# Filling the first microseconds of a transformer-block kernel: dummy matmuls, another load order, the first tile on VectorE, and two token tiles half by half

## The chip, the cores and the metric

The kernel runs on one core of one Trainium2 chip. The metric is the device time of one execution in microseconds (us). Each experiment was timed in five rounds beside the kernel before on the same chip, and it has a ratio with a 95% interval.

## The reference, cut to what matters

```python
h  = x + attention(layernorm(x))          # linear attention with phi(t) = (t + 1 if t > 0 else exp(t)) + 1e-6, then @ wo
h2 = h + (relu(gate) * up) @ W_down       # gate, up = layernorm(h) @ W_gate, W_up
# x: 1 x 2048 x 1024, wqkv: 1024 x 3072, 32 heads of 32, F = 3584, bfloat16
```

Only the first stage matters here: layer normalisation of the first token tiles, and `k = xn @ wk`, `v = xn @ wv` of the first four tiles.

## The kernel before: the parts that the change and the argument touch

A token tile is 128 tokens of 1024 features. Each is loaded, normalised (statistics on VectorE, the scaling on ScalarE), and transposed in eight 128x128 blocks on TensorE. The blocks come in two groups of four. VectorE evicts the first group from PSUM and ScalarE the second; both groups share one PSUM buffer, so the second waits for the first eviction.

```python
load_x(atiles[0])                 # 256 KB
load_w(wk_sb, 0, D)               # first 512 columns of the K weights, 1 MB
load_x(atiles[1])
load_w(wk_sb, 1, D)               # second 512 columns, 1 MB
load_x(atiles[2]); load_x(atiles[3])
for j in range(2):
    load_w(wv_sb, j, 2 * D)

def ln_T(t):
    ...                            # bn_stats x2, bn_aggr, rstd = exp(-0.5 ln(var + eps))
    nc.scalar.activation(out=xn[:], in_=x_sb[:], func=ACT.Identity, bias=nmr, scale=rstd)
    for k in range(2):
        pt = pspool.tile([P, KH, P], BF16, tag="D", bufs=1, name="tp")
        for kc in range(KH):
            nc.tensor.transpose(pt[:, kc, :], xn[:, (k * KH + kc) * P:(k * KH + kc + 1) * P], ident[:])
        (nc.scalar.copy if k else nc.vector.tensor_copy)(
            out=xT[s][i][:, k * KH:(k + 1) * KH, r:r + P], in_=pt[:])

def k_plain(t):
    for j in range(2):             # per column half: 8 matmuls of 128x512, then exp, min, max
        ...

ln_T(atiles[0]); ln_T(atiles[1])
for t in units[0]:                 # four tiles
    k_plain(t)
    ln_T(todo.pop(0))
for n, t in enumerate(units[0]):
    v_plain(t)
    ...
    if n == 1:
        sums_unit(1); k_sums()     # sums of weight blocks for a Strassen-like scheme used later
```

The text of the program isn't the order of the instructions: a scheduler orders each engine's work. It moves `k_sums`, which needs all K weights and nothing else, to the moment when those weights land. It is VectorE work of about 1.2 us per sum.

## Time and profile before

| | |
|---|---|
| median time, 4 runs | 769.04 us (768.19 to 771.18) |
| TensorE busy | 740.3 of 768.0 us |
| first transposes | 7.10 us |
| full rate reached | 14.66 us (first clock record of the trace) |
| first V matmul | 27.74 us |

The page's first part gives busy time of each engine, its share of the span, and instructions:

```profile
PE 740.3 (96%) x3584; PEld 340.2 (44%) x3584; DVE 482.0 (63%) x868; ACT 321.6 (42%) x593; POOL 6.1 (1%) x44
```

TensorE (PE) is the bound, so time can only be won where it idles or runs slowly. The table of waits for the first 32 us says what TensorE waited for (us in total, times, longest):

```profile
PE tp L265 <- ACT xn L258: 7.1, 1, 7.1
PE tp L265 <- DVE xT L266: 1.4, 1, 1.4
PE tp L265 <- ACT xT L266: 0.3, 1, 0.3
```

The timeline of TensorE from 0 to 29 us (start, duration, what, how many; in brackets the idle time before it and what ended it):

```profile
7.10 0.61 PE L265 MATMUL tp<-ident,xn 128*128 128x128 bf16 x4 [7.10 <-ACT xn L258]
9.11 0.58 PE L265 MATMUL tp<-ident,xn 128*128 128x128 bf16 x4 [1.41 <-DVE xT L266]
9.49 1.49 PE L313 MATMUL kp<-pq_mem,xT 128*128 128x512 bf16 x3
11.61 2.77 PE L313 MATMUL kp<-pq_mem,xT 128*128 128x512 bf16 x6
14.60 3.65 PE L313 MATMUL kp<-pq_mem,xT 128*128 128x512 bf16 x16
18.12 0.40 PE L265 MATMUL tp<-ident,xn 128*128 128x128 bf16 x4
27.74 1.46 PE L331 MATMUL vp<-wv_sb,xT 128*128 128x512 bf16 x6
```

Six K matmuls take 2.77 us from 11.61 on, and sixteen take 3.65 us from 14.60 on: the array first runs at half rate. The `tp` groups are the transposes. The matmuls from 18.36 to 27.7 us, left out here, follow each other without a gap.

What stands on VectorE when the second weights land (timeline of VectorE, 9.5 to 12 us), and the traffic of an early stretch (windows view: stretch, length, busy us and instructions of PE, PEld, DVE, ACT and POOL, then clock, DMA share, GB/s):

```profile
10.30 1.23 DVE L127 TENSOR_TENSOR pq_mem<-pq_mem 128x2048 f16<-128x2048 bf16 x1 [0.87 <-DMA pq_mem<-in_A_wqkv_dram]
```

```profile
3.50:6.00 2.50, 0.00 (x0) 0.00 (x0) 1.66 (x4) 0.60 (x3) 0.00 (x0) 1.00 1.09 375
```

The clock of that line, 1.00, isn't to be believed: the views print full rate wherever the trace has no clock record yet, and the first record comes at 14.66 us.

### The profile page before, as it was taken

Reading aid. Unit: us, or ns where it says so; the run is one execution under the profiler, and the core shown is the slowest. Engines: PE = TensorE matmul, PEld = TensorE weight load, DVE = VectorE, ACT = ScalarE, POOL = GpSimd, SP = SyncE. Lnnn points to the kernel's source line nnn. Section 1 sums busy time; section 2 is a strip of 40 time slices with the busy share of each in tenths; the row PEclk is TensorE's granted clock in tenths of the full one; section 3 lists DMA queues with packets and bytes.
Section 4 is the critical chain, followed back from the end, with each engine's and each line's share of the span. In section 5 each row is a group of like instructions: output and inputs, shape, how many; then the busy total and the mean of one; then the engine's idle time right before and its main releaser. Section 6 shows DMA issues by size and latency. Waiting matters only on the chain.

```text
span 768.0 us, 9610 instructions
## 1 busy us (share of the span) xinstructions
PE 740.3 (96%) x3584; PEld 340.2 (44%) x3584; DVE 482.0 (63%) x868; ACT 321.6 (42%) x593; POOL 6.1 (1%) x44
## 2 busy tenths in 40 slices
PE   5999999999889999999999999999998999999998
PEld 2444555444344444444444444444443444444443
DVE  5997654886896766656474564746545991349632
ACT  4775553877777554444444344444434000000000
POOL 0000000000000000000000000000000000000000
PEclk9999999999999999999999999999999999999999
DMA  9675003089767526154032140130001986971001
GB/s 321 145 138 150 1 1 110 1 186 225 180 154 192 121 63 209 45 152 131 7 87 72 34 131 8 55 103 29 28 7 60 331 261 209 316 256 49 28 27 55
DMA packets 125151, 89.76 MB, mean 117 GB/s; under 512 B 50352, under 2 KB 116912, under 8 KB 124592
## 3 DMA queue, kind: packets, MB, share of 16 engines
q1 hardware_dynamic: 125104, 89.15, 40.9%
q8 instruction: 28, 0.46, 0.2%
q14 instruction: 19, 0.16, 0.1%
HBM read 59.77 MB, written 17.83 MB: 101 GB/s over the span
## 4 chain that ended last, share of the span: by engine, by line
PE 64%; DVE 20%; ACT 8%; DMA 4%; issue 3%; SPq 0%; POOL 0%; DVEq 0%; ACTq 0%
PE A L596 16%; PE accA L759 11%; PE E L596 8%; PE accE L759 6%; PE attn L514 4%; DVE gu L615 4%; PE Aq L280 3%; PE Dp L596 3%; PE Aq L414 2%; PE Eq L280 2%; ACT snap L610 2%; PE Aq L629 2%; PE accD L759 2%; DVE stats L249 2%; DMA hn<-hn 1%
## 5 line engine op out<-in xcount | busy, mean ns | idle before, releaser
L615 DVE TENSOR_TENSOR gu<-E,snap 128x1024 bf16<-128x1024 f32 x48 | 58.7, 1223 | 90.1 <-ACT snap L610 87.5
L610 ACT COPY snap<-A 128x1024 f32<-128x1024 f32 x72 | 72.0, 1008 | 84.1 <-PE A L596 84.1
L759 PEld LDWEIGHTS <-hh 128*128 128x128 bf16 (+1 forms) x560 | 54.7, 98 | 67.7 <-issue 1.9
L617 ACT ACTIVATE gu<-gu 128x512 bf16<-128x512 bf16 x72 | 45.4, 630 | 86.2 <-DVE gu L615 85.9
L759 PE MATMUL accA<-wd,hh 128*128 128x512 f16 (+1 forms) x336 | 73.3, 379 | 1.4 <-DVE gu L615 1.4
L514 PE MATMUL attn<-wo_mem,oT 128*128 128x512 bf16 x256 | 59.3, 385 | 3.4 <-DVE o_sb L494 3.1
L596 PEld LDWEIGHTS <-tg 128*128 128x128 f16 x384 | 37.5, 98 | 49.5 <-issue 5.7
L596 PEld LDWEIGHTS <-tu 128*128 128x128 f16 x384 | 37.6, 98 | 45.3
L618 DVE TENSOR_TENSOR hh<-gu 128x512 bf16<-128x512 bf16 x72 | 30.5, 423 | 38.4 <-ACT gu L617 38.4
L147 ACT COPY u<-Aq 128x512 f32<-128x512 f32 x56 | 32.2, 581 | 44.5 <-PE Aq L280 20.9
L596 PE MATMUL A<-hn,tg 128*128 128x512 f16 (+1 forms) x192 | 49.3, 379 | 1.1 <-ACT snap L610 1.1
L596 PE MATMUL A<-hn,tu 128*128 128x512 f16 (+1 forms) x192 | 49.3, 379 | 0.0
L596 PEld LDWEIGHTS <-wg 128*128 128x128 bf16 x288 | 28.2, 98 | 34.5 <-issue 1.1
L596 PEld LDWEIGHTS <-wu 128*128 128x128 bf16 x288 | 28.2, 98 | 34.0
L514 PEld LDWEIGHTS <-oT 128*128 128x128 bf16 x256 | 25.2, 99 | 36.0 <-issue 8.6
L759 PEld LDWEIGHTS <-s 128*128 128x128 f16 x224 | 21.9, 98 | 27.2 <-issue 0.8
L615 DVE TENSOR_TENSOR gu<-Dp,snap 128x1024 bf16<-128x1024 f32 x24 | 29.3, 1220 | 2.3 <-PE Dp L596 2.3
L280 PEld LDWEIGHTS <-xT 128*128 128x128 bf16 (+1 forms) x192 | 18.6, 98 | 23.9 <-issue 2.4
L767 DVE TENSOR_TENSOR u<-accA,hres 128x512 f32<-128x512 f32 x16 | 10.8, 690 | 28.6 <-PE accA L759 28.1
L494 DVE TENSOR_TENSOR o_sb<-nd,rd 128x384 bf16<-128x384 f32 (+1 forms) x48 | 22.9, 508 | 8.6 <-ACT rd L493 8.3
L516 DVE SCALAR_TENSOR_TENSOR x_res<-attn,x_res 128x512 bf16<-128x512 f32 x32 | 22.0, 688 | 7.7 <-PE attn L514 7.6
L596 PE MATMUL E<-hs,tg 128*128 128x512 f16 x96 | 24.6, 378 | 0.9
(161 smaller groups left out, 1217.5 us busy)
## 6 DMA issues: line engine op xcount, KB each, us to landing
wd<-in_B_W_down_dram SPq DMA_DIRECT2D x16, 896.0 KB, 6.5
hh_dram<-hh SPq DMA_DIRECT2D x72, 128.0 KB, 1.7
wg<-in_B_W_gate_dram SPq DMA_DIRECT2D x14, 512.0 KB, 4.9
wu<-in_B_W_up_dram SPq DMA_DIRECT2D x14, 512.0 KB, 4.9
hh<-hh_dram SPq DMA_DIRECT2D x4, 1792.0 KB, 8.0
x_sb<-in_A_x_dram SPq DMA_DIRECT2D x16, 256.0 KB, 3.8
x_res<-in_A_x_dram SPq DMA_DIRECT2D x16, 256.0 KB, 3.0
h_dram<-x_res SPq DMA_DIRECT2D x16, 256.0 KB, 2.6
```

The source lines that it names most:

```text
L147: nc.scalar.copy(out=snaps[nm, v], in_=A[v][:])
L249: nc.vector.bn_stats(out=stats[:, k, :], in_=x_sb[:, k * NW:(k + 1) * NW])
L280: nc.tensor.matmul(ps[:], lhsT=left[m - 1][:, kc, r + v * P:r + (v + 1) * P], rhs=right[m - 1][:, kc, :], start=(start and kc == 0), stop= ...
L494: nc.vector.tensor_tensor(out=ov[:, c0:c0 + n], in0=ndv[:, :, 0:P].rearrange("p k (h e) -> p k h e", h=HPC), in1=rd[:, 0:n, :].unsqueeze(3 ...
L514: nc.tensor.matmul(ps[:], lhsT=st["oT"][:, c, :], rhs=wo_sb[:, c, j * NW:(j + 1) * NW], start=(c == 0), stop=(c == KC - 1))
L516: nc.vector.scalar_tensor_tensor(out=h_sb[:, j * NW:(j + 1) * NW], in0=ps[:], scalar=1.0, in1=h_sb[:, j * NW:(j + 1) * NW], op0=ALU.mult, ...
L596: nc.tensor.matmul(ps[:, v, :], lhsT=w[v][m - 1][:, kc, :], rhs=left[m - 1][:, kc, :], start=(start and kc == 0), stop=(kc == KH - 1), ski ...
L610: nc.scalar.copy(out=m[:], in_=ps[:])
L615: nc.vector.tensor_tensor(out=gu[:], in0=ps[:], in1=m[:], op=ALU.add)
L617: nc.scalar.activation(out=gu[:, 0, :], in_=gu[:, 0, :], func=ACT.Relu)
L618: nc.vector.tensor_tensor(out=d, in0=gu[:, 0, :], in1=gu[:, 1, :], op=ALU.mult)
L759: nc.tensor.matmul(accs[tt][:], lhsT=lhs[:, half * FD + f, tt * P:(tt + 1) * P], rhs=rhs[half][:, f, :], start=(start and half == 0 and f ...
```

## The change

Its intent: warm the array with dummy matmuls while the loads fly, have two token tiles on the chip before the weights, shorten the first tile's way by normalising it on VectorE in halves, and do tiles 0 and 1 column half by column half, so that the second weights are needed later. The core of the diff:

```diff
-        load_w(wk_sb, 0, D)
         load_x(atiles[1])
+        load_w(wk_sb, 0, D, KH)          # in two loads of 512 KB
         load_w(wk_sb, 1, D)
...
+            if t == atiles[0]:
+                for k in range(2):
+                    ks = slice(k * NW, (k + 1) * NW)
+                    nc.vector.tensor_scalar(out=xn[:, ks], in0=x_sb[:, ks], scalar1=mv[:, 0:1], scalar2=rstd,
+                                            op0=ALU.subtract, op1=ALU.mult)
+                transpose_in(t, xn)
+                return
...
-        ln_T(atiles[0])
+        with tc.high_priority():
+            zero = asmall.tile([P, NW], BF16, tag="zero", bufs=1, name="zero")
+            nc.vector.memset(zero[:], 0.0)
+            spin = pspool.tile([P, NW], FP32, tag="E", bufs=2, name="spin")
+            for n in range(SPIN):         # 14
+                nc.tensor.matmul(spin[:], lhsT=zero[:, 0:P], rhs=zero[:], start=True, stop=True)
+            ln_T(atiles[0])
         ln_T(atiles[1])
-        for t in units[0]:
-            k_plain(t)
-            ln_T(todo.pop(0))
+        first = [(t, (j,)) for j in range(2) for t in units[0][:2]] + [(t, (0, 1)) for t in units[0][2:]]
+        for t, js in first:
+            k_plain(t, js)
+            if js[0] or len(js) == 2 or t == units[0][1]:
+                ln_T(todo.pop(0))
```

More of the change, by code (lines that the diff above doesn't have):

```diff
@@ L74, in block_kernel @@
     PE_T = 4
+    SPIN = 14
     XB, HB = 3, 2
@@ L220, in load_x, with load_w @@
             x_tiles[t] = x_sb
-        def load_w(dst, j, col):
-            nc.sync.dma_start(out=dst[:, :, j * NW:(j + 1) * NW], in_=wqkv_v[:, :, col + j * NW:col + (j + 1) * NW])
+        def load_w(dst, j, col, step=KC):
+            for k in range(0, KC, step):
+                nc.sync.dma_start(out=dst[:, k:k + step, j * NW:(j + 1) * NW],
+                                  in_=wqkv_v[:, k:k + step, col + j * NW:col + (j + 1) * NW])
         def place(t):
@@ L261, in ln_T, with transpose_in @@
                 return
+            transpose_in(t, xn)
+        def transpose_in(t, xn):
+            s, i, r = place(t)
             for k in range(2):
@@ L303, in k_unit, with k_plain @@
             return token_unit(u, rk, fin)
-        def k_plain(t):
+        es = {}
+        def k_plain(t, cols):
             s, i, r = place(t)
-            new_pk(t)
-            e = bwork.tile([P, D], BF16, tag="o_sb", name="e")
-            for j in range(2):
+            if t not in pk:
+                new_pk(t)
+                es[t] = bwork.tile([P, D], BF16, tag="o_sb", name="e")
+            e = es[t]
+            for j in cols:
                 js = slice(j * NW, (j + 1) * NW)
```

## The prediction

> **What bounds the kernel now.** The page's engine table has TensorE busy 740.3 of 768.0 us (96%), VectorE 63%, so only TensorE's idle or slow time can be saved. The table of waits shows it at the start: 7.1 us before the first transpose, 1.4 and 0.3 us on evictions of transposes. The timeline adds that until about 14.2 us matmuls run slowly: six 128x512 K matmuls take 2.77 us from 11.61 (0.43 us apart), sixteen take 3.65 us from 14.60 (0.22). "TensorE: Matmul & The Clock Gate" of the Trainium skill (section on the clock gate) says the array runs at half rate until about 3.4 us of sustained work; this trace agrees. From 14.6 us TensorE is full until about 45 us; V starts at 27.74 us. By 14.6 it has done 9 K matmuls and 16 transposes, about 3.5 us at full rate: some 11 us is start-up loss. Not all can go: weights arrive at about 350 GB/s (windows view), first half near 7.2 us, second near 10.3 us (VectorE's first sum of weights starts then).
>
> **What the change does.**
> - 14 dummy matmuls from about 1 us: 8 slow (3.4 us), the rest fast, done by 6 to 7 us, in idle time. Worth up to 2 us of the slow part of 9.5 to 14.4, if the array stays warm through later gaps.
> - The second token tile lands near 4.4 instead of 7.2 us; weights as before.
> - First tile on VectorE: two halves of about 0.3 us (estimate from the 128x512 tensor_scalar, 0.29 us) for one ScalarE pass of 1.24 us. But the built order puts half a bn_stats of tile 1 (0.65 us) ahead of tile 0's aggregate, and ScalarE's 1.24 us pass for tile 1 ahead of its eviction of tile 0's second transposes. First transposes at about 6.6 us (7.1 before), first K matmuls at 8.5 (9.5 before).
> - Half by half does not fill the gap: in the built order three matmuls of tile 0's second column half stand before tile 1's first half. They wait for the second weights (10.3 us), and VectorE stands in its 1.23 us weight sum, also from 10.3, ahead of an eviction of tile 1's transposes. Tile 1's remaining transposes start near 12 us.
>
> I walked the built order with durations of the trace: tile 1's K work runs at full speed from about 12.4 to 16.9; tile 2 is transposed at about 17.3 (18.1 before), with 32 K matmuls done (25 before). Then tile 2's second transposes wait about 0.6 us on VectorE (a weight sum is in front), with no K matmul left as filler. V starts near 26.4 instead of 27.7: 1.3 us gained. VectorE is 97% busy from 40 to 60 us and gets 0.6 us more work, so a little may be given back. After that the order is nearly unchanged and the gain passes to the end.
>
> **Prediction.** 768.3 us, 1.2 us (0.2%) less; range 765.8 to 770.2. Chances: faster by over 2% 0.005, within 2% 0.99, slower by over 2% 0.005.
>
> **What would show it.** K matmuls 0.22 us apart from the first; first transposes at 6 to 7 us; a TensorE gap at about 11 to 12 us behind VectorE's sum or the second weights; another near 17 to 18.5 around tile 2; V starting at 26 to 27 us; TensorE waits after 60 us unchanged.
>
> **What would make it wrong.** The array cooling again at 6 to 12 us (1 to 2 us lost); VectorE giving all back by 60 us; or weights landing earlier, so that tile 1 isn't held up and 3 to 4 us are gained.

## The result, and the profile after

The changed kernel took 771.23 us in the median of 4 runs (769.93 to 771.85), against 769.04 us before. The ratio is 1.0023, interval [1.0005, 1.0041]: the same at 2%, and slightly longer where the prediction said 1.2 us shorter. The time lies outside the predicted range. (A ratio is the mean time of one kernel's runs over that of the other's of the same rounds, so it isn't quite the ratio of the medians that are quoted.)

TensorE's waits in the first 32 us, after:

```profile
PE tp L279 <- DVE xT L280: 1.9, 3, 0.9
PE kp L331 <- DMA pq_mem<-in_A_wqkv_dram: 1.7, 1, 1.7
PE spin L384 <- DVE zero L381: 1.2, 1, 1.2
```

The wait of 7.1 us for the first normalised tile is gone, and a wait of 1.7 us for weights is new. The timeline of TensorE shows where both led:

```profile
1.19 6.03 PE L384 MATMUL spin<-zero 128*128 128x512 bf16 x14 [1.19 <-DVE zero L381]
7.05 0.39 PE L279 MATMUL tp<-ident,xn 128*128 128x128 bf16 x4
8.17 1.03 PE L331 MATMUL kp<-pq_mem,xT 128*128 128x512 bf16 x4
9.41 1.03 PE L331 MATMUL kp<-pq_mem,xT 128*128 128x512 bf16 x4
12.12 0.81 PE L331 MATMUL kp<-pq_mem,xT 128*128 128x512 bf16 x3 [1.68 <-DMA pq_mem<-in_A_wqkv_dram]
13.78 0.58 PE L279 MATMUL tp<-ident,xn 128*128 128x128 bf16 x4 [0.86 <-DVE xT L280]
14.16 6.20 PE L331 MATMUL kp<-pq_mem,xT 128*128 128x512 bf16 x21
20.45 0.40 PE L279 MATMUL tp<-ident,xn 128*128 128x128 bf16 x4
21.36 0.38 PE L279 MATMUL tp<-ident,xn 128*128 128x128 bf16 x4 [0.52 <-DVE xT L280]
28.98 0.38 PE L349 MATMUL vp<-wv_sb,xT 128*128 128x512 bf16 x1
```

The first K matmuls run at full rate and 1.3 us earlier than before (8.17 against 9.49). Then TensorE idles from 10.44 to 12.12 us for the second weights, and from 12.93 to 13.78 us for an eviction on VectorE. Then 21 matmuls take 6.20 us. At the full-rate distance of 0.2155 us they would take 4.53; so about 1.67 us are lost while nothing is waited for. The windows view shows why, in its clock column (third from the right):

```profile
3.50:6.00 2.50, 2.50 (x7) 0.90 (x6) 2.50 (x6) 0.41 (x2) 0.00 (x0) 1.00 0.83 251
10.36:13.78 3.42, 0.89 (x4) 0.29 (x3) 1.61 (x3) 0.60 (x1) 0.00 (x0) 1.00 1.08 360
13.78:17.19 3.41, 3.41 (x12) 1.45 (x12) 3.20 (x7) 0.79 (x2) 0.00 (x0) 0.50 1.09 349
17.19:20.60 3.41, 3.32 (x18) 1.42 (x17) 2.34 (x6) 2.62 (x6) 0.00 (x0) 1.00 0.90 321
```

From 13.78 to 17.19 us the granted clock was 0.50. The 3.4 us before it held three K matmuls. The first line, from 3.5 to 6.0 us, shows another thing: the loads moved 251 GB/s there, against 375 before. And VectorE's first weight sum moved with the weights from 10.30 to 12.17 us. It still stands ahead of the eviction that TensorE needs at 12.93:

```profile
12.17 1.23 DVE L128 TENSOR_TENSOR pq_mem<-pq_mem 128x2048 f16<-128x2048 bf16 x1 [4.27 <-DMA pq_mem<-in_A_wqkv_dram]
13.31 0.42 DVE L280 COPY xT<-tp 128x512 bf16<-128x512 bf16 x1
```

V starts at 28.98 us, 1.24 us later than before. At 80 us the work as a whole lags by 1.15 us (starts of the same ScalarE and VectorE instructions in both traces), and at the end by 2.02. Of the further loss 0.3 us falls between 205 and 230 us, and 0.5 us near 270 us, where a wait of 1.5 us grew. The waits from 255 to 290 us, before and then after:

```profile
PE Aq L629 <- ACT m L147: 1.5, 1, 1.5
```

```profile
PE Aq L655 <- ACT m L148: 2.0, 1, 2.0
```

### The profile page after: what moved, and what is told of

It is laid out like the page before. It is cut to its first block, busy times and chain, and to the rows that moved or that the text cites. A ratio compares the mean times of both kernels' runs of the same rounds, so it can differ in the third digit from the quotient of the medians.

```text
span 770.0 us, 9640 instructions
## 1 busy us (share of the span) xinstructions
PE 746.0 (97%) x3598; PEld 341.7 (44%) x3598; DVE 482.1 (63%) x870; ACT 320.6 (42%) x592; POOL 5.9 (1%) x44
## 4 chain that ended last, share of the span: by engine, by line
PE 65%; DVE 19%; ACT 8%; DMA 4%; issue 3%; SPq 0%; POOL 0%; DVEq 0%; ACTq 0%
PE A L622 16%; PE accA L785 11%; PE E L622 8%; PE accE L785 6%; PE attn L540 5%; DVE gu L641 4%; PE Aq L294 3%; PE Dp L622 3%; PE Aq L440 2%; PE Eq L294 2%; PE Aq L655 2%; ACT snap L636 2%; PE accD L785 2%; DMA hn<-hn 1%; ACT hn L552 1%
```

## The experiments

I had these theories of the 2 us (and of the 3 us that were missing against the prediction):

1. The second weights land late because of the new load order (1.8 us late in the trace).
2. The clock: the array is put back to half rate for one window of 3.41 us.
3. The order: half by half leaves TensorE without work to put between transposes.
4. The order on VectorE: a weight sum stands ahead of an eviction.
5. Splitting the first weight load in two is what delays the loads.

(The expectations further down number their theories in their own way; go by what they say, not by the number.)

In the sixteen runs, "before + X" starts from the kernel before, "change - X" from the changed kernel. The table is the summary; times are medians, those of before from the same chip. "Second weights" is when the first and the last of that load's 16 parts landed in the profiled execution (from the semaphore updates in the packed trace; no view prints them).

| run | edit | us (before) | ratio, 95% | second weights, us | V starts |
|---|---|---|---|---|---|
| before | | 769.04 | 1 | 9.88 to 10.21 | 27.74 |
| the change | | 771.23 (769.04) | 1.0023 [1.0005, 1.0041] | 10.12 to 12.08 | 28.98 |
| again | the change, repeated | 768.82 (769.53) | 0.9993 [0.9975, 1.0010] | 11.05 to 11.58 | 26.82 |
| after3 | the change, repeated | 770.29 (769.59) | 1.0009 [0.9990, 1.0028] | 10.08 to 11.92 | 28.85 |
| nosplit | change - split load | 770.25 (769.53) | 1.0009 [0.9992, 1.0027] | 10.29 to 12.53 | 27.8 |
| nospin | change - dummies | 772.38 (769.53) | 1.0036 [1.0020, 1.0053] | to 12.20 | 30.2 |
| dve_order | change, weight sums held back | 772.03 (769.53) | 1.0030 [1.0011, 1.0048] | to 12.29 | 28.7 |
| b_spin | before + dummies | 767.32 (769.05) | 0.9973 [0.9956, 0.9991] | 9.81 to 10.24 | 25.58 |
| b_x1first | before + tile 1 ahead of the weights | 770.15 (769.05) | 1.0018 [0.9997, 1.0039] | 9.99 to 10.98 | 27.1 |
| fill | dve_order + 8 dummies | 773.14 (769.05) | 1.0056 [1.0034, 1.0079] | to 11.16 | 29.9 |
| xfirst2 | four token tiles first | 771.29 (769.05) | 1.0027 [1.0005, 1.0049] | to 12.24 | other order |
| oldload | change, old load order | 771.26 (770.13) | 1.0021 [1.0004, 1.0039] | to 10.31 | 26.63 |
| s_half | before + dummies + half by half | 770.63 (770.13) | 1.0017 [1.0000, 1.0034] | 9.88 to 11.10 | 28.6 |
| b_split | before + split load | 770.15 (770.13) | 1.0014 [0.9992, 1.0037] | 10.02 to 10.55 | 27.6 |
| whole | change - half by half | 769.08 (769.59) | 0.9996 [0.9981, 1.0012] | 10.69 to 12.61 | 28.86 |
| s_dve | before + dummies + VectorE tile | 768.41 (769.59) | 0.9984 [0.9970, 0.9999] | 9.89 to 10.23 | 25.57 |
| best | s_dve + two orders on VectorE | 767.41 (770.13) | 0.9969 [0.9953, 0.9986] | to 10.43 | 25.18 |
| best2 | best, repeated | 767.65 (769.59) | 0.9974 [0.9960, 0.9987] | 9.85 to 11.12 | 26.78 |

All outputs are right.

### The change again, unchanged: again and after3

> The changed kernel unchanged, to see what repeats. Theory 1 (the split of the first weight half upsets the transfers): the 16 parts of that load again land 1.5 to 2 us apart and the second weights again near 12 us. Rival: that was an accident of one execution, and the second weights land near 10.3 us as before. The array cooled once at 13.8 us for 3.4 us in the traced execution (mean clock 0.996) and two of four executions show 0.998 instead: I expect the same mixture, 0.996 executions about 1 to 1.7 us longer than 0.998 ones. Ratio to the kernel before 1.001 to 1.004.

> The change again, unchanged, beside the other three on one chip. It had 1.0023 and 0.9993 in two earlier sets. If the half-rate window near 14 us comes in some executions and not in others, its executions fall on both sides of 770 us, those with clock 0.996 about 1.5 to 2 us longer than those with 0.998; its mean lies 1 to 3 us above the best kernel's.

Three sets of the same kernel gave 1.0023, 0.9993 and 1.0009. The intervals overlap, so there is no contradiction, but the first set was the worst of the three. The 16 runs together have a median of 769.96 us and a mean of 770.0; the 44 runs of before in the four later sets have a mean of 769.5 (48 with those of the result, the same mean). So the change is about 0.5 us slower, or equal, and doesn't gain what was predicted.

The profiled execution of again had a clock of 1.000 and no half-rate window at all. Its TensorE timeline comes near to what was predicted:

```profile
11.62 0.81 PE L331 MATMUL kp<-pq_mem,xT 128*128 128x512 bf16 x3 [1.00 <-DMA pq_mem<-in_A_wqkv_dram]
13.28 0.38 PE L279 MATMUL tp<-ident,xn 128*128 128x128 bf16 x4 [0.86 <-DVE xT L280]
13.50 4.70 PE L331 MATMUL kp<-pq_mem,xT 128*128 128x512 bf16 x20
18.29 0.40 PE L279 MATMUL tp<-ident,xn 128*128 128x128 bf16 x4
19.20 0.38 PE L279 MATMUL tp<-ident,xn 128*128 128x128 bf16 x4 [0.52 <-DVE xT L280]
26.82 2.54 PE L349 MATMUL vp<-wv_sb,xT 128*128 128x512 bf16 x11
```

The same instructions in the same order: V starts 2.16 us earlier than in the other trace of this kernel. Of these, 1.67 us are the half-rate window, and 0.50 us are weights that landed at 11.58 instead of 12.08. Together that is 2.17. So theory 2 is shown for the trace of the result, by two executions of one kernel. In the times it shows as clusters: of the 16 runs the six with clock 1.000 took 768.6 us in the mean, and the four with 0.995 or 0.996 took 772.1. At clock 1.000 the 23 such runs of before took 768.8, so without half-rate windows change and before are alike within 0.2 us. The mean clocks of all runs are 0.9981 and 0.9989; the difference is worth about 0.7 us (an estimate, explained at theory 3), as much as the 0.5 us between the means.

One caution: the mean clock is that of the whole execution. Most of the traces, before's too, have one more half-rate window between 203 and 212 us, where TensorE idles for VectorE, and in again, s_half, b_split and best2 it didn't come.

Whether the window comes is partly luck, because the phase of the windows isn't tied to the program. "TensorE: Matmul & The Clock Gate" of the Trainium skill (Part 1, "What's actually happening") says that the window is 4096 cycles, about 3.41 us, and free-running. The traces agree: every half-rate stretch in the middle of a trace lasts 3.41 us, and with the same 14 dummies full rate came anywhere from 3.94 us (after3) to 7.14 us (whole).

### When the array is put back to half rate

Counting the work in each window of 3.41 us between the first full rate and about 25 us gives a table. I counted matmuls (0.215 us each) and transposes (0.055 us each, both as the starts at full rate lie apart), as shares of the window. These are all windows at full rate with less than 0.47 of matmuls:

| run, window (us) | matmuls | transposes | next window |
|---|---|---|---|
| dve_order 15.97 to 19.39 | 0.00 | 0.06 | half |
| fill 16.89 to 20.30 | 0.13 | 0.06 | half |
| nospin 11.01 to 14.42 | 0.13 | 0.06 | half |
| the change 10.36 to 13.78 | 0.19 | 0.00 | half |
| whole 10.55 to 13.97 | 0.19 | 0.00 | half |
| s_half 7.42 to 10.84 | 0.25 | 0.06 | half |
| best2 8.14 to 11.55 | 0.31 | 0.00 | half |
| nosplit 5.83 to 9.24 | 0.19 | 0.13 | half |
| after3 10.77 to 14.18 | 0.31 | 0.06 | half |
| b_spin 6.62 to 10.03 | 0.31 | 0.13 | full |
| xfirst2 4.70 to 8.11 | 0.31 | 0.13 | full |
| s_dve 6.96 to 10.37 | 0.31 | 0.13 | full |
| oldload 4.47 to 7.89 | 0.38 | 0.06 | full |
| five others | 0.44 | 0.06 to 0.13 | full |

By matmuls alone 0.31 stands on both sides. With the transposes counted, every window up to 0.37 was followed by half rate and every one from 0.44 on by full rate. This is a sorting of what was seen, not a test made for it, and the border isn't sharp. Counted in the same way to the end of all 18 traces, where TensorE has no transposes (matmuls narrower than 512 columns counted by their width), every window with up to 0.33 of matmuls led to half rate (twelve, all near 205 us) and every one from 0.41 on to full rate. But of those at 0.38 to 0.40, four led to half rate (after3 and whole near 205 us, oldload and best2 near 270) and nine to full. (A few matmul records are missing in the traces, so a share can be 0.06 too low.) Still, it says what the dummies buy: not a warm array for good, only full rate until the first window that's too empty. The page's section "Why this matters for your kernels" warns of idle gaps above about 3 us between bursts. Here gaps of 1.68 and 0.86 us, in one window of 3.41, were enough.

### Theories 5 and 1: nosplit, b_split, b_x1first

```diff
-        load_w(wk_sb, 0, D, KH)         # nosplit: the change, one load
+        load_w(wk_sb, 0, D)
```
```diff
-        load_w(wk_sb, 0, D)             # b_split: before, with the first weights in two loads of 512 KB
+        for k in range(0, KC, KH):
+            nc.sync.dma_start(out=wk_sb[:, k:k + KH, 0:NW], in_=wqkv_v[:, k:k + KH, D:D + NW])
```
```diff
-        load_w(wk_sb, 0, D)             # b_x1first: before, with tile 1 ahead of the weights
         load_x(atiles[1])
+        load_w(wk_sb, 0, D)
```

> First weight half loaded in one piece, still behind the second token tile. Theory 1 (the split delays weights): the second weights land at 10.3 to 10.6 us instead of 12.1, VectorE's first sum starts then, V starts 1 to 2 us earlier than 28.98, ratio to before 0.999 to 1.001. Rival (the split is innocent): landing near 12 us again and no change of V's start beyond 0.5 us.

> The kernel before with its first weight half loaded in two pieces, order otherwise as before. Theory 5 (what delays is small loads in front: a third load whose 16 parts are not all there when the first two, small ones, are through): the first two loads are now 0.25 and 0.5 MB instead of 0.25 and 1, through at about 4.4 us, so a spread of the parts between 0.5 and 1.5 us appears in the third load. Rival (only two token tiles in a row do it, or the split is harmless): spread stays below 0.5 us and second weights complete at 10.2 us. Ratio 0.999 to 1.002.

> The kernel before with the second token tile loaded ahead of the first weight half, in one piece, nothing else. Theory 1b (that order, not the split, makes the weights' 16 parts land 1.5 to 2.6 us apart): the last part of the first weights at 9 us or later (7.3 expected by bytes) and the second weights complete at 11.5 to 12.5 us (10.21 before); ratio to before 1.000 to 1.003. Rival (something else in the change does it): spread below 0.5 us and second weights at 10.2 us, ratio 0.999 to 1.000.

Without the split the second weights were as late as with it (12.53 us), and before with the split had them at 10.55. So theory 5 falls. With tile 1 in front the second weights' last part came at 10.98 instead of 10.21, and in all ten traces of kernels with two or more token tiles in front it came at 10.98 us or later, up to 12.61. In six of the eight with the old order it came at 10.21 to 10.55. But s_half and best2, in the old order, had 11.10 and 11.12; the order makes the delay likely and isn't its only cause. In time theory 1 isn't resolved: b_x1first has 1.0018, but its interval includes 1 and reaches 1.0039; whole and s_dve, which differ in the loads alone, have 0.9996 and 0.9984, overlapping; and oldload, with its second weights at 10.31, was no faster than the change.

In the trace of the result what is late is the last part, not the load as a whole: after the change the parts of the second weights land from 10.12 to 12.08 us, before from 9.88 to 10.21. In again, the same kernel, it is the load as a whole: its parts land close together, from 11.05 to 11.58. "DMA: Bandwidth & Descriptors" of the skill ("Queues, rings and completion order") says that a copy is split over up to 16 engines' rings and that completion isn't in order of issue. The traces agree in that each load has 16 parts that land on their own, up to 2.6 us apart (the first weights of nosplit from 6.94 to 9.52 us). What drives the parts apart when two small loads are in front stays open; no run here looked into it. From 6 to 17 us both kernels move 348 to 367 GB/s in the windows view, so what the change lost from 3.5 to 6.0 us isn't made good there.

### What the dummies do: nospin, b_spin

nospin takes these lines out of the change; b_spin puts only them into the kernel before:

```diff
+            zero = asmall.tile([P, NW], BF16, tag="zero", bufs=1, name="zero")
+            nc.vector.memset(zero[:], 0.0)
+            spin = pspool.tile([P, NW], FP32, tag="E", bufs=2, name="spin")
+            for n in range(14):
+                nc.tensor.matmul(spin[:], lhsT=zero[:, 0:P], rhs=zero[:], start=True, stop=True)
```

> No dummy matmuls, all else of the change. In this build the order on TensorE changes too: tile 1's first column half stands ahead of tile 0's second. Theory 2 (the dummies warm the array but make the scheduler order TensorE badly, so that a gap behind the second weights cools it again): slow matmuls until 13 to 15 us but no long gap, no second cooling, V starting at 27 to 29 us; ratio to before 0.999 to 1.003, so no worse than the whole change. Rival (dummies are worth their 2 us): 1 to 2 us slower than the whole change, 1.004 to 1.006.

> The kernel before with the 14 dummy matmuls alone. If the dummies are what helps: array at full rate by 5.3 to 7.2 us, second weights at 9.9 to 10.3 us as before, V starts at 26 to 27 us (27.74 before), ratio to before 0.998 to 0.9995. Rival (waiting for tiles takes it all back, or the array cools in a gap): V starts at 27.5 us or later, ratio 1.000 or more.

The dummies alone are worth 0.27%, about 2 us. The change without them is the slower by about as much (1.0036, against 1.0008 for the mean of the change's three sets), though its build orders TensorE's work differently too (tile 1's first column half ahead of tile 0's second), so that difference isn't the dummies' alone. The 2 us of b_spin are what the prediction allowed the dummies ("up to 2 us"). In b_spin the array is at full rate from 6.62 us on, and V starts at 25.58:

```profile
12.57 3.83 PE L313 MATMUL kp<-pq_mem,xT 128*128 128x512 bf16 x16
25.58 3.62 PE L331 MATMUL vp<-wv_sb,xT 128*128 128x512 bf16 x16
```

So one part of the change had the whole gain that one could hope for, and the others took it away again.

### Theory 4: dve_order and fill

```diff
+        evicted = {}                      # filled where VectorE evicts a tile's first transposes
...
-                k_sums()
+                with tc.issue_after(evicted[atiles[1]].ins):
+                    k_sums()
```

`issue_after` makes the scheduler place what it holds behind the given instruction on the engine. With it, the matmuls get the order on TensorE that the text of the change suggests: the first column half of both tiles ahead of the second. fill adds eight dummies behind tile 1's K work, to keep the array at full rate, and holds tile 2's transposes behind them (that hold isn't shown):

```diff
+                fill = pspool.tile([P, NW], FP32, tag="A", bufs=2, name="fill")
+                with tc.issue_after(mms["last"].ins):        # the last K matmul of tile 1
+                    for n in range(FILL):                    # 8
+                        mms["fill"] = nc.tensor.matmul(fill[:], lhsT=zero[:, 0:P], rhs=zero[:], start=True, stop=True)
```

> The whole change, with VectorE's first weight sum held behind its eviction of tile 1's first transposes. The build then puts tile 1's first column half ahead of tile 0's second, as the change meant. Theory 2: the gap of 3.3 us on TensorE between 10.4 and 13.8 us shrinks below 1.5 us, the array stays warm to 60 us, V starts at 26 to 27 us instead of 28.98, ratio to before 0.997 to 0.999. Rival (the loss is in the transfers alone, or VectorE bounds the stretch to V): V starts at 28 us or later, ratio 1.001 to 1.003.

> As dve_order, with 8 more dummy matmuls between tile 1's last K matmul and tile 2's transposes, where dve_order's array stood idle 2.5 us and cooled. Theory 3 (the clock is taken away in a window of 3.41 us with little TensorE work, and a half-rate window costs 1.7 us): no half-rate window from the first full rate to 60 us, mean clocks 0.002 higher than dve_order's in most executions, ratio to before 0.999 to 1.001, that is 1.5 us or more better than dve_order. Rival (idle time itself is the loss, clock a by-product): ratio stays within 0.5 us of dve_order's.

dve_order loses as much as the change or more (1.0030). The stall at 12 us went away, and a longer one came at 16 us: with all K work of two tiles done early, TensorE has nothing left and waits for tile 2 to be normalised.

```profile
18.46 0.40 PE L281 MATMUL tp<-ident,xn 128*128 128x128 bf16 x4 [2.48 <-ACT xn L268]
```

fill was to show that the half-rate window is what this costs. It failed: the dummies ran directly behind the K work, as the edit held them, VectorE was late with an eviction (behind another weight sum), and TensorE idled after the dummies instead of before.

```profile
15.75 1.89 PE L403 MATMUL fill<-zero 128*128 128x512 bf16 x8
17.48 0.39 PE L283 MATMUL tp<-ident,xn 128*128 128x128 bf16 x4
20.99 0.58 PE L283 MATMUL tp<-ident,xn 128*128 128x128 bf16 x4 [3.12 <-DVE xT L284]
```

The next window (20.30 to 23.71) was at half rate all the same. This run tells nothing about what a window is worth.

### More token tiles in front: xfirst2

xfirst2 loads four token tiles before any weights, does all four half by half, and holds the weight sums back further:

```diff
-        load_x(atiles[1])
-        load_w(wk_sb, 0, D, KH)
+        for t in atiles[1:4]:
+            load_x(t)
+        load_w(wk_sb, 0, D)
...
+        for j in range(2):
+            for t in units[0]:
+                k_plain(t, (j,))
+                if j:
+                    ln_T(todo.pop(0))
```

> Tries to beat both: all four first token tiles loaded ahead of the weights, K column half by half over all four tiles, weight sums of VectorE held behind the evictions of the first tiles, dummies kept. Theory: with all four tiles normalised while weights fly there is K work from the first weights (8 to 9 us) without a gap over 1 us, no half-rate window after the dummies up to 60 us, V starts at 24.5 to 26 us, ratio to before 0.995 to 0.998. Rival (VectorE and ScalarE bound this stretch, so TensorE's early start is given back before 60 us): ratio 0.999 or more.

At 26.95 us it had all K work and eight V matmuls done, which before had at 29.46, so it was 2.5 us ahead; by 110 us all of that was gone, to waits for VectorE and ScalarE (TensorE waits 3.0 us for copies of `m` in its first 130 us, against 1.0 before). Filling the start better doesn't help where the engines behind can't follow.

### Theory 3, half by half: oldload, s_half, whole, s_dve

oldload is the change with the load order of before. s_half has the first tile on ScalarE besides, and that tile's `ln_T` is no longer inside the block of high priority:

```diff
+        load_w(wk_sb, 0, D)             # oldload and s_half
         load_x(atiles[1])
-        load_w(wk_sb, 0, D, KH)
...
-            if t == atiles[0]:          # s_half only: the VectorE branch is taken out
-                ...
-                return
```

whole and s_dve take half by half out, with the new and with the old loads:

```diff
-        first = [(t, (j,)) for j in range(2) for t in units[0][:2]] + [(t, (0, 1)) for t in units[0][2:]]
+        first = [(t, (0, 1)) for t in units[0]]
```

> The whole change with the load order and the unsplit load of the kernel before. Theory 4 (the moved second token tile is the part that costs: it delays the weights; dummies give about 2 us): 16 parts of each load within 0.5 us again, second weights complete at 10.2 us, V starts at 25.3 to 26.3 us, ratio to before 0.996 to 0.9985, like the dummies alone (0.9973). Rival (the half by half order or VectorE's first tile cost something of their own): 0.999 or more.

> Kernel before, its load order, dummies and the half by half order, first tile normalised on ScalarE as before. The order of the build on TensorE is the same as oldload's, so the difference from oldload is VectorE's first tile alone: by the trace 1.24 us of ScalarE against 0.74 of VectorE, but the first transposes' eviction waits behind tile 1's statistics at 8.6 us in either. Expected ratio within 0.0007 of oldload's; 0.996 to 0.9985.

> The change without its half by half part: dummies, both token tiles ahead of the weights, weights of K in two loads for the first half, first tile on VectorE, but each tile's K work in one piece as before. In the built order tile 2's two blocks of transposes again have three K matmuls between them as filler, where the change has none. Theory A (half by half itself costs, by leaving no filler for tile 2's transposes): about 2 us less than the change, ratio to before 0.998 to 1.000. Theory B (what the change loses is the late second weights and the half-rate window they bring, and the order matters little): as the change, 1.001 to 1.003, and the trace shows the second weights' last part at 11.5 us or later.

> The kernel before with its load order, plus dummies and the first tile normalised on VectorE, tiles whole: it differs from the run with the old loads in nothing but half by half, and from the run with dummies alone only in the VectorE tile. Theory A (half by half costs): 0.997 to 0.998, as the dummies alone; V starts at 25.2 to 26.0 us. Theory B (half by half is neutral; the run with old loads and the one with ScalarE lost to clock windows by chance): 1.001 to 1.002.

With the old loads, half by half costs: 1.0021 [1.0004, 1.0039] with it and 0.9984 [0.9970, 0.9999] without. The intervals don't overlap; the difference is about 2.8 us. One part of it is in the traces. Between the two groups of a tile's transposes oldload has four K matmuls and then waits 0.96 us for an eviction:

```profile
17.93 0.38 PE L279 MATMUL tp<-ident,xn 128*128 128x128 bf16 x4
18.15 1.03 PE L331 MATMUL kp<-pq_mem,xT 128*128 128x512 bf16 x4
20.14 0.38 PE L279 MATMUL tp<-ident,xn 128*128 128x128 bf16 x4 [0.96 <-ACT xT L280]
```

s_dve has eight at the same place, and doesn't wait:

```profile
17.80 0.38 PE L279 MATMUL tp<-ident,xn 128*128 128x128 bf16 x4
18.02 1.89 PE L331 MATMUL kp<-pq_mem,xT 128*128 128x512 bf16 x8
19.94 0.38 PE L279 MATMUL tp<-ident,xn 128*128 128x128 bf16 x4
```

V starts 1.06 us later for it (26.63 against 25.57). The other part is clock: the runs of oldload have a mean clock of 0.9958, those of s_dve 0.9980. A window at half rate for a time T costs T/2 and lowers the mean clock by T/2 over the span, so the missing clock times the span is the loss: 0.0022 of 770 us, 1.7 us. The two together are 2.7 us, near the 2.8 measured, but that is partly luck. In the two traces the lag has grown from 1.06 us at V's start to 2.0 us at 80 us, with no half-rate window between: TensorE waits 1.7 us for ScalarE's copies of `m` from 27 to 80 us in oldload, 0.4 in s_dve. And the two sets ran on two chips, whose runs of before had mean clocks of 0.9987 and 0.9994; against these the missing clock is 0.0015, or 1.2 us. The second part stands on a clock rounded to three digits in six runs each; it is an estimate. Why half by half brought more windows isn't settled either. In oldload's trace they lie at 206 and 274 us, not at the start. A second pair has the same step with the first tile on ScalarE: s_half with half by half 1.0017 [1.0000, 1.0034], b_spin without 0.9973 [0.9956, 0.9991], apart again. In both pairs the two sets are of different chips, but best, which is without half by half too (and has two holds on VectorE, below), stood beside oldload and s_half in one set and has 0.9969. So the cost of half by half with the old loads is shown, and how it divides is not.

With the new loads the same step is smaller and not resolved: whole has 0.9996 [0.9981, 1.0012], after3 on the same chip 1.0009 [0.9990, 1.0028]. In their profiled executions, both with late weights and a half-rate window, V starts at the same moment (28.86 and 28.85 us).

The VectorE tile is worth nothing that could be measured: oldload and s_half, with and without it, are alike (1.0021 and 1.0017), and so are s_dve and b_spin (0.9984 and 0.9973, overlapping).

### A version that beats both: best and best2

Dummies and the VectorE tile, the old loads, whole tiles, and two holds on VectorE: tile 1's statistics behind the eviction of tile 0's first transposes, and the weight sums behind that of tile 1's.

```diff
+        with tc.issue_after(evicted[atiles[0]].ins):
+            ln_T(atiles[1])
...
+                with tc.issue_after(evicted[atiles[1]].ins):
+                    k_sums()
```

> Tries to beat both: old load order, dummies, first tile on VectorE, whole tiles; VectorE's statistics of tile 1 held behind the eviction of tile 0's first transposes, and its weight sums behind tile 1's first eviction. First K matmuls at about 7.5 us instead of 9.5; no half-rate window from the first full rate to 60 us. Expected V at 24.5 to 25.5 us, ratio 0.9955 to 0.9975, 0.3 to 1 us better than the dummies alone. Rival (VectorE gives it back, as in xfirst2): same as the dummies alone or worse.

> The best kernel so far again, unchanged, on this chip: 0.9953 to 0.9986 if its gain of 0.3 per cent is of the kernel, about 1.000 if it was luck with the clock windows.

It was 0.31 and 0.26% faster than before in two sets on two chips; neither interval includes 1. All ten runs lie at or below 768.8 us. It isn't distinguishable from the dummies alone (0.9973) or from s_dve (0.9984); so the holds may be worth nothing, and of the parts that it has, only the dummies were shown to gain. It can be cooled too. In best2's profiled execution the weights came at 11.12 us, TensorE waited 2.1 us, and the next window was at half rate:

```profile
8.14:11.55 3.41, 1.29 (x7) 0.48 (x5) 1.41 (x4) 1.84 (x4) 0.00 (x0) 1.00 1.08 365
11.55:14.97 3.42, 3.42 (x15) 1.71 (x14) 3.15 (x8) 0.42 (x2) 0.00 (x0) 0.50 1.09 348
```

## Why the prediction was wrong, and where it was right

- **Failed: "second near 10.3 us" for the weights.** The prediction took the landing times of before as unchanged ("weights as before"). With two token tiles in front they landed at 12.08 us in the trace of the result, and at 11.58 to 11.92 in the repeats: a term mis-sized by 1.3 to 1.8 us. (The first half, "near 7.2", was complete at 9.07.) A load's order was changed, and its time was then read from the trace of the old order.
- **Failed: "tile 1's K work runs at full speed from about 12.4 to 16.9".** It ran from 14.16 to 20.4, and at half rate until 17.19. The cooling was named ("the array cooling again at 6 to 12 us, 1 to 2 us lost"), but as a risk and not in the sum. It came at 13.78 and cost 1.67 us. A gap of 1.3 to 2 us was predicted for just that stretch, so the window should have been priced in, at least with even odds: two of the change's three profiled executions had it.
- **Failed, smaller: "the gain passes to the end".** 0.5 us was lost near 270 us, in again too, which was 1.23 us ahead at 80 us. Why that wait of 1.5 us became 2.0 was not tested. In the 18 traces it runs from 1.1 (b_x1first) to 2.1 us (oldload, best2), and it is long in best too (1.9), so it doesn't follow the kernels' speed.
- **Mis-sized at the start, without effect:** "8 slow, the rest fast, done by 6 to 7 us". In the trace all 14 dummies were slow (6.03 us). The first window that they filled entirely ran from 3.54 to 6.95 us, when full rate came, and the first transposes waited behind them until 7.05 instead of 6.6.
- **Right:** the first K matmuls at about 8.5 us (8.17); the stall behind weights and VectorE's sum (10.44 to 13.78, for weights that came later); the wait of 0.6 us at tile 2's second transposes (0.52); "half by half does not fill the gap". Given no half-rate window, V at 26.4 us was near: 26.82 in again.

The sum on V's start: from the predicted 26.4 to the measured 28.98 are 2.6 us. 1.8 of late weights and 1.67 of half rate make 3.5, so the walk had counted 0.9 us too much elsewhere: about 0.3 from tile 1's to tile 2's transposes (5.3 predicted, 6.67 less 1.67 measured), and 0.6 from there to V (9.1 against 8.53).

Seen from the experiments, the larger omission is another: the change was costed as one sum. Costed by parts, the dummies alone would have stood out as worth 2 us (0.9973) and half by half, by the prediction's own words without a filler for tile 2, as a loss.

## What to carry to other kernels

Dummy matmuls during the first loads are worth their six lines, but what they buy lasts only until the first 3.41-us window in which TensorE has little to do: price each expected gap after them that leaves such a window with less than about 0.4 of work at up to 1.7 us on top of itself. Moving a small load ahead of a large one can move the landing of everything behind both, here by 0.8 to 2.4 us though the bytes in front of the second weights were the same: read the last part of each load in a trace of the new order. And when tiles are pipelined, work finished early is filler missing later: before doing two tiles' matmuls first, look at what TensorE will have to do between the third tile's two groups of transposes.

## What the Trainium skill lacked or had wrong

- "TensorE: Matmul & The Clock Gate", Part 1 and "Why this matters for your kernels": the pages speak of an idle window, or of gaps above about 3 us. (A section of Part 1, on the second failure mode, has frequent short idle times between groups of matmuls, without an amount.) In these runs windows that weren't idle were enough: in the first 25 us all nine with matmuls and transposes together at 0.06 to 0.37 of the window led to half rate, and none from 0.44 on did; later on both were seen from 0.38 to 0.40. Two gaps of 1.68 and 0.86 us in one window sufficed.
- The same page, Part 4 on the transpose, says that transposes don't count as busy in the same way. Here 0.31 of matmuls led to half rate with 0.00 and 0.06 of transposes, and not with 0.13 (three times). That fits transposes that do count; it wasn't tested apart, and later windows without transposes went both ways at one share too (0.38). The clock reaches transposes in any case: they start 0.107 us apart in the half-rate window after the change and 0.055 at full rate.
- The same page, on warming up: it budgets about 3.4 us, and one busy window, and doesn't say how busy; its note of 6 to 14 slow matmuls by the phase of the window fits these runs better. With 14 dummies from 1.19 us on, full rate came between 3.94 and 7.14 us, 2.8 to 6.0 us after the first; a window that was busy for 0.69 of its length (0.12 to 3.54 us after the change) or 0.74 (0.31 to 3.73 in whole) wasn't enough, and one of 0.81 (0.53 to 3.94 in after3) was.
- "DMA: Bandwidth & Descriptors": nothing says how far the 16 parts of one load can land apart. It was 0.33 us for the second weights before and up to 2.2 us with token tiles in front (2.6 for the first weights), and a consumer waits for the last.
- The same page's "Specifications" give a limit of about 358 GB/s from HBM per core; before the change the trace has 378 GB/s from 4 to 6 us and 385 from 18 to 20, so this one-core program went up to 8% above it in stretches; in the stretch from 13.78 to 17.19 us it stays just under it (352 before, 349 after).
